# A first x tile loaded entirely by DMA transposes, with W1's row blocks on a second queue

## The chip, the cores and the metric

The kernel runs on one core of one Trainium2 chip. The metric is the device time of one execution in microseconds (us). A core has a matrix engine (TensorE, PE in the profile; its weight loads are the row PEld), a vector engine (VectorE, DVE), an engine for activation functions (ScalarE, ACT), GpSimd (POOL) and SyncE (SP). SyncE, ScalarE and GpSimd each issue DMA transfers from a queue of their own, in program order. An engine runs its own instructions in order too, and waits on semaphores for those of others.

## The reference

The input x has 2048 tokens of 640 features, all in bf16. Three things are computed from it and mixed.

```python
g = _sigmoid((x * gate_w).sum(-1, keepdims=True))
# a: a state space model
dt = jnp.exp(log_dt)
Lam_bar = jnp.exp(dt * Lam)
B_bar = ((Lam_bar - 1.0) / Lam)[:, None] * Bmat
Bu = jnp.einsum("bld,pd->blp", x + 0j, B_bar)
for t in range(L):
    h = Lam_bar[None, :] * h + Bu[:, t, :]
y = 2.0 * jnp.einsum("blp,dp->bld", hseq, Cmat).real + x * Dskip[None, None, :]
# b: a dense layer, GELU, a dense layer
h = _gelu(jnp.einsum("bsd,df->bsf", x, w1) + b1)
b = jnp.einsum("bsf,fd->bsd", h, w2) + b2
return g * a + (1 - g) * b
```

The state has 640 complex values, and w1 is 640 x 1728.

## The kernel before, in words

The tokens are cut into four tiles of 512 (q = 0 to 3). For every tile, x is wanted transposed, with features on the 128 partitions: `xT[q]` holds five slabs (k = 0 to 4) of 128 features x 512 tokens. The other layout, `xn`, has tokens on the partitions, and is used for the gates and for the output.

TensorE does the matrix products: `m1` (x by W1, L670), `bproj` (x by B, L713), `outsT` (the GELU's result by W2, L937, and the state by C, L986), and for the last tile `outs` (L800 and L849). ScalarE applies GELU and moves results out of PSUM, the eight banks that TensorE writes. VectorE builds tables from Lambda and dt, runs the recurrence in blocks of 256 tokens (`ssm`, a scan in L753) and does the final mixing.

The first product, `m1_first` (L648), is special, because nothing is there yet when the kernel starts. It takes the first eight column groups of W1 (jf = 0 to 7, 128 columns each, FW = 1024 columns together), one in each bank, and goes through the features slab by slab: all groups of slab 0, then of slab 1, and so on, 40 products of 128x512, so that it can start with one slab of x and one row block of W1 (`w1load`, 128 x 1024, 256 KB). The product for group 7 of slab 0 stands late in slab 1, because its bank is first used by a small transposition (`cols`, L454). That one turns `rows`, in which the small vectors Lambda, log_dt and b1 lie as rows, into columns; the tables on VectorE and the bias of GELU need it. Its sources are five small loads on ScalarE's queue (`lre`, `lim`, `ldt`, `b1a`, `b1b`).

Ahead of all this, seven products on a constant (`warm`, L415) keep TensorE at work while the first data is on its way.

In the kernel before, slabs 0 and 1 of the first tile come as they lie in memory (`xna`, L369, the first issue of SyncE's queue, 256 KB). TensorE transposes them against an identity matrix (L427, eight instructions of 128x128), VectorE copies the result to `xT[0]` (L433, four copies), and two short products on a constant (`fill`, L440) cover the copies. The first two products are cut in halves of 256 tokens, so that they can start after the first copy. Slabs 2, 3 and 4 are loaded by DMA transposes (`xtrans`, L353), which write `xT[0]` directly. These and all of W1's row blocks stand in SyncE's queue, alternating; the blocks of slabs 1 and 3 are cut in two (WSPLIT). Behind them come the rest of W1 (`w1_r`), B, the other x tiles, W2 and C.

The order of instructions is found by a planner at build time: each operation names its engine, an assumed duration, what it reads and writes, and a priority (lower goes first among what is ready). The planner walks through assumed time and writes one fixed order for each engine. It does not see the chip; a change to one assumed duration or priority can move an instruction in the order.

Of the kernel before, what the change touches and what calls it, by code (L numbers as in the profile page):

```python
# [9 lines left out]
BF16 = mybir.dt.bfloat16  # L10
# [137 lines left out]
class Prog:  # L148
# [8 lines left out]
    def op(self, name, eng, dur, reads, writes, fn, prio=None, lat=0.0, after=()):  # L157
        deps = {}
        for k in reads:
            for w in self.last_w.get(k, ()):  # L160
                deps[w.idx] = w
        for k in writes:
            for w in self.last_w.get(k, ()):
                deps[w.idx] = w
            for r in self.last_r.get(k, ()):
                deps[r.idx] = r
        for a in after:
            deps[a.idx] = a
        deps = list(deps.values())
        E = self.E  # L170

        def run(eg, deps=deps, eng=eng, fn=fn):
            E.wait(eng, *[d.done for d in deps if not (eng == "pe" and d.eng == "pe")])
            return fn()

        it = self.sch.add(name, eng, dur, deps, run, prio=prio, lat=lat)
        for k in writes:
            self.last_w[k] = [it]
            self.last_r[k] = []
        for k in reads:  # L180
            self.last_r.setdefault(k, []).append(it)
        return it


def bass_gated_mix__ssm_conv_s5__dense_activation_gelu__prompt_kernel(
# [18 lines left out]
    _, S, D = A_x.shape  # L204
    P = A_Lambda_re.shape[0]
    F = B_w1.shape[1]
    assert S % 512 == 0 and D % 128 == 0 and P == D
    KD = D // 128
# [6 lines left out]
    FL = F - (NF - 1) * 128  # L215
# [6 lines left out]
    x2 = A_x[0]  # L222
# [3 lines left out]
    with ExitStack() as es:  # L226
# [4 lines left out]
        xT = [SB(f"xT_{i}", [128, KD, 512], BF16) for i in range(NQ)]  # L231
        xn = [SB(f"xn_{i}", [128, 4, D], BF16) for i in range(2)]
        W1sb = SB("W1sb", [128, KD, F], BF16)
# [20 lines left out]
        ident = SB("ident", [128, 128], BF16)  # L254
# [39 lines left out]
        PS = [es.enter_context(nc.psum_tensor(f"ps{i}", [128, 512], FP32)) for i in range(8)]  # L294
# [13 lines left out]
        op = pr.op  # L308

        def inc(eng, ins):  # L310
            return E.inc(eng, ins, eng + "_s")
# [14 lines left out]
        def d_mm(n):  # L326
            return n / 2400.0 + 0.004


        def load(name, eng, sem, dst, src, writes, prio, dur=0.5, lat=2.5, reads=(), after=()):  # L330
            def fn():
                with nc.allow_non_contiguous_dma(reason="columns of small vectors"):
                    return dma_inc(eng, engines[eng].dma_start(dst, src), sem)
            return op(name, eng, dur, reads, writes, fn, prio=prio, lat=lat, after=after)
# [9 lines left out]
        def xnload(q, eng, prio=None):  # L344
            load(f"xn{q}", eng, f"l_xn{q}", xn[q % 2][:, :, :],
                 x2[q * 512:(q + 1) * 512, :].rearrange("(c p) d -> p c d", p=128),
                 [("xn", q % 2, 0), ("xn", q % 2, 1)], prio, dur=1.0, lat=6.0)

        NW = 8
        FW = NW * 128  # L350
        nmain = (NF - 1) * 128

        def xtrans(q, ks, prio, dur):  # L353
            load_T(f"xT{q}_{ks[0]}", f"l_xT{q}_{ks[0]}", [(xT[q][:, ks[0]:ks[-1] + 1, :], x2[q * 512:(q + 1) * 512, ks[0] * 128:(ks[-1] + 1) * 128])],
                   [("xT", q, k) for k in ks], prio, dur)

        WSPLIT = {1: 6, 3: 6}

        def w1load(k, eng, prio):
            edges = [0] + ([WSPLIT[k] * 128] if k in WSPLIT else []) + [FW]  # L360
            for i, (f0, f1) in enumerate(zip(edges, edges[1:])):
                load(f"w1_{k}{i}", eng, f"l_w1{k}{i}", W1sb[:, k, f0:f1], B_w1[k * 128:(k + 1) * 128, f0:f1], [("w1", k, i)], prio=prio + 0.1 * i, lat=2.6)

        def w1tok(k, jf):
            return ("w1", k, int(jf >= WSPLIT.get(k, NW)))

        KN = 2

        load("xna", "sp", "l_xna", xn[0][:, :, 0:KN * 128], x2[0:512, 0:KN * 128].rearrange("(c p) d -> p c d", p=128), ["xna"], 0, dur=0.45, lat=2.0)  # L369
        w1load(0, "sp", 1)  # L370
        w1load(1, "sp", 1.3)
        xtrans(0, range(KN, KN + 1), 1.6, 0.8)
        w1load(2, "sp", 2)
        xtrans(0, range(3, 4), 3, 0.8)
        w1load(3, "sp", 4)
        xtrans(0, range(4, 5), 4.5, 0.8)
        w1load(4, "sp", 5)
        FM = FW + 3 * 128
        for i, (f0, f1) in enumerate(((FW, FM), (FM, F))):
            load(f"w1_r{i}", "sp", f"l_w1r{i}", W1sb[:, :, f0:f1], B_w1[:, f0:f1].rearrange("(k p) f -> p k f", p=128), [("w1", "r", i)], prio=20 + i, lat=5.0)  # L380
# [8 lines left out]
        for i, (nm, (r0, src)) in enumerate(ROWS.items()):  # L389
            src = src.rearrange("(k p) -> k p", p=128)  # L390
            load(nm, "act", "l_" + nm, rows[r0:r0 + src.shape[0], :], src, [nm], prio=-100 + i, dur=0.4)
        load("b1b", "act", "l_b1b", rows[RT:RT + 1, :].rearrange("o (a p) -> o a p", a=2),
             B_b1[nmain:F].rearrange("(o p) -> o p", o=1).unsqueeze(1).broadcast_to([1, 2, FL]), ["b1b"], prio=-101, dur=1.2)

        def f_iota():
            inc("pool", nc.gpsimd.iota(io_i[:, :], pattern=[[1, 128]], base=0, channel_multiplier=-1))
# [14 lines left out]

        def f_warm():
            t = None
            for n in (512,) * 6 + (256,):
                t = nc.tensor.matmul(PS[4][:, 0:n], one.broadcast_to([128, 128]), one.broadcast_to([128, n]), start=True, stop=True)  # L415
            return inc("pe", t)

        op("warm", "pe", 2.7, (), [("bank", 4)], f_warm, prio=-1000)

        for i, (k, c0, c1) in enumerate(((0, 0, 2), (0, 2, 4), (1, 0, 2), (1, 2, 4))):  # L420
            bank = (7, 6, 5, 4)[i]
            pt = PS[bank][:, :].bitcast(BF16)[:, 0:(c1 - c0) * 128]

            def f_xt(k=k, pt=pt, c0=c0, c1=c1):
                t = None
                for c in range(c0, c1):
                    t = nc.tensor.transpose(pt[:, (c - c0) * 128:(c - c0 + 1) * 128], xn[0][:, c, k * 128:(k + 1) * 128], ident[:, :])  # L427
                return inc("pe", t)

            op(f"xt{i}", "pe", 0.11 * (c1 - c0), ["xna", "ident"], [("bank", bank)], f_xt, prio=-990 + i)  # L430

            def f_xc(k=k, pt=pt, c0=c0, c1=c1):
                return inc("dve", nc.vector.tensor_copy(out=xT[0][:, k, c0 * 128:c1 * 128], in_=pt))  # L433

            op(f"xc{i}", "dve", 0.42, [("bank", bank)], [("xT", 0, k, c0)], f_xc, prio=-2000 + i)

        def f_fill():
            t = None
            for _ in range(2):
                t = nc.tensor.matmul(PS[3][:, 0:256], one.broadcast_to([128, 128]), one.broadcast_to([128, 256]), start=True, stop=True)  # L440
            return inc("pe", t)

        op("fill", "pe", 0.22, ["xna", "ident"], [("bank", 3)], f_fill, prio=-900)

        XK0 = [[("xT", 0, k)] for k in range(KD)]
        XK0[0] = [("xT", 0, 0, 0), ("xT", 0, 0, 2)]
        XK0[1] = [("xT", 0, 1, 0), ("xT", 0, 1, 2)]
        XT = {q: [("xT", q, k) for k in range(KD)] for q in range(1, NQ)}
        XT[0] = [t for x in XK0 for t in x]

# [137 lines left out]
        for ci, src in enumerate((A_B_re, A_B_im)):  # L588
            for i, (p0, p1) in enumerate(((0, 512), (512, KP * 128))):
                load_T(f"B{ci}{i}", f"l_B{ci}{i}", [(BT[:, ci, :, p0:p1], src[p0:p1, :])], [("BT", ci, i)], prio=30 + ci + 0.1 * i, dur=0.8 * (p1 - p0) / 128)  # L590
        xtrans(1, range(KD), 32, 3.4)
        load("gwb", "sp", "l_gwb", gwb[:, :], gate_w.partition_broadcast(128), ["gwb"], prio=32.2)
        load("xnb", "sp", "l_xnb", xn[0][:, :, KN * 128:D], x2[0:512, KN * 128:D].rearrange("(c p) d -> p c d", p=128),
             [("xn", 0, 0), ("xn", 0, 1)], 32.4, dur=1.0, lat=6.0, reads=["xna"])
        big = load("w2a", "sp", "l_w2a", W2sb[:, 0:NF - 1, :], B_w2[0:nmain, :].rearrange("(j p) d -> p j d", p=128), ["w2a"], prio=33, lat=8.0)
        load("w2b", "sp", "l_w2b", W2sb[0:FL, NF - 1, :], B_w2[nmain:F, :], ["w2b"], prio=34, lat=4.0)
        load("w2c", "sp", "l_w2c", W2sb[64:64 + FL, NF - 1, :], B_w2[nmain:F, :], ["w2c"], prio=34.2, lat=4.0)
# [12 lines left out]
        def pe_prio():  # L610
            ctr["pe"] += 1
            return ctr["pe"]
# [26 lines left out]
        def m1_first():  # L639
            seq = [(k, jf) for k in range(KD) for jf in range(NW)]  # L640
            seq.remove((0, NW - 1))
            seq.insert(seq.index((1, NW - 1)), (0, NW - 1))
            steps = [(0, 0, 0), (0, 1, 0), (0, 0, 1), (0, 1, 1)] + [(k, jf, None) for k, jf in seq if k or jf > 1]
            for k, jf, h in steps:
                t0, t1 = (0, 512) if h is None else (256 * h, 256 * h + 256)

                def f_mm(jf=jf, k=k, t0=t0, t1=t1):
                    return inc("pe", nc.tensor.matmul(PS[jf][:, t0:t1], W1sb[:, k, jf * 128:(jf + 1) * 128], xT[0][:, k, t0:t1],  # L648
                                                      start=(k == 0 and t0 == 0), stop=(k == KD - 1), skip_group_check=jf < 2))

                op(f"m1_0_{jf}_{k}_{t0}", "pe", d_mm(t1 - t0), (XK0[k] if h is None else XK0[k][h:h + 1]) + [w1tok(k, jf)], [("bank", jf)],
                   f_mm, prio=pe_prio())
            for jf in range(NW):
                ctr["bank"] += 1

                def f_ge(jf=jf):
                    return inc("act", nc.scalar.activation(Gl[0][:, jf, :], PS[jf][:, :], ACT.Gelu_apprx_tanh, bias=b1col[:, jf:jf + 1]))

                op(f"ge_0_{jf}", "act", d_act(512), [("bank", jf), "b1col"], [("gl", 0, jf)], f_ge, prio=10)
# [442 lines left out]
```

## Time and profile before

| | us |
|---|---|
| runs, median of 3 | 213.17 (213.05 to 213.45) |
| profiled execution, first to last instruction (span) | 211.2 |
| TensorE busy | 208.4 (99%) |
| VectorE busy | 190.2 (90%) |
| ScalarE busy | 102.9 (49%) |
| first stage L648, start and end | 4.59 and 13.61 |

The page gives the profiled execution by its span alone; the runs' median is 1.97 us above it. A row of a timeline or of a chain has the start (us from the span's start), the length (us), the engine, and the line of the kernel with what it writes and, after "x", how many instructions are merged. "SPq" and "ACTq" are the queues in which SyncE and ScalarE issue transfers; the length of such a row is the time for issuing, and the time from issue to landing is in a list of its own. In a table by stretches of time, the last three columns are the clock granted to TensorE, the share of time in which DMA packets were under way (it can be over 1), and the GB/s that they moved.

### The profile page before, as it was taken

What the parts mean: (1) busy time and instruction counts of PE and PEld (TensorE: products, weight loads), DVE (VectorE), ACT (ScalarE), POOL (GpSimd) and SP (SyncE); (2) the same over time, 40 slices, a digit from 0 to 9 for tenths busy, and PEclk for the clock granted to TensorE, in tenths of its full rate; (3) what the DMA queues carried; (4) which work ended last, traced back from release to release, by engine and by line L of the source; (5) the groups of instructions that cost most, each with busy time, mean ns of one, the idle gap of its engine ahead of it and who ended that gap; (6) DMA issues with size and microseconds to landing.
All of it is one profiled execution on the core that took longest, in us unless ns stands there. A gap on an engine that the chain in (4) does not pass through costs nothing.

```text
span 211.2 us, 2755 instructions
## 1 busy us (share of the span) xinstructions
PE 208.4 (99%) x1104; PEld 104.3 (49%) x1104; DVE 190.2 (90%) x240; ACT 102.9 (49%) x177; POOL 4.2 (2%) x12
## 2 busy tenths in 40 slices
PE   8999999999999999999999999999999999999996
PEld 3444444444554444444464444444456444567775
DVE  2599999999999999999999999899999999499744
ACT  2588556672990453556680073456660037622330
POOL 1000000030000000000100000000010000000000
PEclk9999999999999999999999999999999999999999
DMA  6899999999930010066074000009542000005251
GB/s 168 203 255 139 193 154 204 310 218 180 218 81 4 0 50 0 0 95 146 10 59 115 3 0 0 0 2 104 114 99 108 0 3 0 0 0 107 69 138 64
DMA packets 48808, 19.08 MB, mean 90 GB/s; under 512 B 41500, under 2 KB 47772, under 8 KB 48796
## 3 DMA queue, kind: packets, MB, share of 16 engines
q1 hardware_dynamic: 47136, 17.59, 41.3%
q0 software_dynamic: 1600, 1.32, 4.5%
q8 instruction: 8, 0.13, 0.3%
q10 hardware_dynamic: 60, 0.01, 0.1%
q14 instruction: 4, 0.03, 0.1%
HBM read 8.41 MB, written 2.63 MB: 52 GB/s over the span
## 4 chain that ended last, share of the span: by engine, by line
PE 99%; DVE 0%; issue 0%
PE ps L670 22%; PE ps L713 20%; PE ps L937 20%; PE ps L986 15%; PE ps L800 7%; PE ps L849 5%; PE ps L648 4%; PE ps L415 1%; PE ps L691 1%; PE ps L948 1%; PE ps L814 0%; PE ps L427 0%; DVE W1sb L883 0%; PE ps L440 0%; PE ps L454 0%
## 5 line engine op out<-in xcount | busy, mean ns | idle before, releaser
L670 PE MATMUL ps<-xT,W1sb 128*128 128x512 bf16 x220 | 48.1, 379 | 0.0
L753 DVE TENSOR_TENSOR_SCAN W<-atab,V 128x1280 bf16<-128x1280 f32 x16 | 44.3, 2812 | 0.3
L713 PE MATMUL ps<-xT,BT 128*128 128x512 bf16 x200 | 43.8, 379 | 0.0
L937 PE MATMUL ps<-Gl,W2sb 128*128 128x512 bf16 (+1 forms) x234 | 42.7, 344 | 0.0
L677 ACT ACTIVATE Gl<-ps,cols 128x512 bf16<-128x512 f32 x44 | 29.9, 694 | 15.5 <-PE ps L670 15.5
L670 PEld LDWEIGHTS ps<-xT,W1sb 128*128 128x128 bf16 x220 | 21.5, 98 | 26.0
L986 PE MATMUL ps<-Hb,CT 128*128 128x512 bf16 x150 | 32.9, 379 | 0.0
L937 PEld LDWEIGHTS ps<-Gl,W2sb 128*128 128x128 bf16 x234 | 22.9, 98 | 19.3
L713 PEld LDWEIGHTS ps<-xT,BT 128*128 128x128 bf16 x200 | 19.5, 98 | 23.8 <-ACT Gt L699 0.4
L722 ACT ACTIVATE U<-ps 128x512 bf16<-128x512 f32 x40 | 23.5, 600 | 14.4 <-PE ps L713 14.3
L955 ACT ACTIVATE E1T<-ps,cols 128x512 bf16<-128x512 f32 (+1 forms) x18 | 9.5, 623 | 33.6 <-PE ps L948 33.6
L986 PEld LDWEIGHTS ps<-Hb,CT 128*128 128x128 bf16 x150 | 14.5, 98 | 17.9 <-DVE V L504 0.6
L994 ACT ACTIVATE E2T<-ps 128x512 bf16<-128x512 f32 x15 | 9.1, 604 | 13.6 <-PE ps L986 13.6
L800 PE MATMUL ps<-W2sb,Gl 128*128 128x320 bf16 x104 | 14.8, 299 | 0.0
L623 DVE SCALAR_TENSOR_TENSOR trf<-xn,gwb 128x640 bf16<-128x640 bf16 x16 | 13.2, 823 | 0.4
L504 DVE TENSOR_TENSOR Hb<-Hb,V 128x1280 bf16<-128x1280 bf16 x16 | 12.5, 822 | 0.3
L504 DVE TENSOR_TENSOR V<-V,W 128x1280 bf16<-128x1280 bf16 x16 | 12.5, 821 | 0.3
L504 DVE TENSOR_TENSOR V<-mr,U 128x2560 bf16<-128x2560 bf16 x8 | 11.9, 1492 | 0.3
L800 PEld LDWEIGHTS ps<-W2sb,Gl 128*128 128x128 bf16 x104 | 10.1, 98 | 4.3 <-issue 0.3
L504 DVE TENSOR_TENSOR Hb<-c,W 128x2560 bf16<-128x2560 bf16 x8 | 11.9, 1490 | 0.2
L974 ACT ACTIVATE xT<-xT,cols 128x512 bf16<-128x512 bf16 x15 | 10.1, 740 | 4.0 <-DMA cols<-in_A_Dskip_dram 4.0
L504 DVE TENSOR_TENSOR W<-mi,U 128x2560 bf16<-128x2560 bf16 x8 | 11.9, 1484 | 0.0
(93 smaller groups left out, 152.0 us busy)
## 6 DMA issues: line engine op xcount, KB each, us to landing
W2sb<-in_B_w_dram SPq DMA_DIRECT2D x1, 2080.0 KB, 9.0
out_dram<-xn SPq DMA_DIRECT2D x3, 640.0 KB, 4.8
xn<-in_A_x_dram POOLq DMA_DIRECT2D x2, 640.0 KB, 7.2
W1sb<-in_B_w_dram SPq DMA_DIRECT2D x3, 256.0 KB, 3.1
trf<-grow SPq DMA_DIRECT2D x3, 256.0 KB, 5.1
xn<-in_A_x_dram SPq DMA_DIRECT2D x1, 640.0 KB, 7.2
W1sb<-in_B_w_dram SPq DMA_DIRECT2D x1, 480.0 KB, 4.0
out_dram<-W1sb SPq DMA_DIRECT2D x3, 160.0 KB, 1.8
```

Of the source, the lines that this page charges most:

```text
L504: return inc("dve", nc.vector.tensor_tensor(out=o, in0=a, in1=b, op=o_))
L623: t = inc("dve", nc.vector.scalar_tensor_tensor(out=scr[:, :], in0=xn[q % 2][:, c, :], scalar=1.0, in1=gwb[:, :], op0=ALU.mult, op1=ALU.mu ...
L670: t = nc.tensor.matmul(PS[bank][:, :], W1sb[:, k, jf * 128:(jf + 1) * 128], xT[q][:, k, :], start=(k == 0), stop=(k == KD - 1))
L677: return inc("act", nc.scalar.activation(Gl[q % 2][:, jf, :], PS[bank][:, :], ACT.Gelu_apprx_tanh, bias=b1col[:, jf:jf + 1]))
L713: t = nc.tensor.matmul(PS[bank][:, :], BT[:, ci, kd, k * 128:(k + 1) * 128], xT[q][:, kd, :], start=(kd == 0), stop=(kd == KD - 1))
L722: return inc("act", nc.scalar.activation(dst, src, ACT.Copy, scale=1.0 if ci == 0 else -1.0))
L753: t = inc("dve", nc.vector.tensor_tensor_scan(out=g[:, ci, :], data0=a, data1=v[:, ci, :], initial=0.0, op0=ALU.mult, op1=ALU.add))
L800: t = nc.tensor.matmul(PS[bank][:, 0:HALF], Gl[q % 2][:, jf, t4 * 128:(t4 + 1) * 128], W2sb[:, jf, cols], start=False, stop=False, skip_gr ...
L849: t = nc.tensor.matmul(PS[bank][:, 0:n], H[b % NHB][:, ci, k, s * 128:(s + 1) * 128], CT[:, ci, k, cols], start=(i == 0), stop=(i == 2 * K ...
L937: t = nc.tensor.matmul(PS[bank][:, 0:t1 - t0], W2sb[:, jf, d * 128:(d + 1) * 128], Gl[q % 2][:, jf, t0:t1], start=(jf == 0), stop=False)
L974: return inc("act", nc.scalar.activation(xT[q][:, d, :], xT[q][:, d, :], ACT.Copy, scale=cols2[:, 1, d:d + 1]))
L986: t = nc.tensor.matmul(PS[bank][:, :].rearrange("p (s t) -> p s t", s=2), CT[:, ci, k, d * 128:(d + 1) * 128], Hb[:, 2 * (q % 2):2 * (q % ...
```

## The change

All five slabs of the first x tile are loaded by DMA transposes from SyncE's queue: three single slabs, then slabs 3 and 4 in one transfer. They are the first four issues of that queue. `xna`, the transposes on TensorE, the copies on VectorE, the filler and the halves are gone; the first stage has 40 whole products. W1's row blocks are whole (no WSPLIT) and go to ScalarE's queue. Its order is now: W1 blocks 0 and 1, `lre`, `lim`, `ldt`, `b1a`, W1 block 2, `b1b`, W1 blocks 3 and 4. The last product of the warm-up has 512 columns where it had 256. The later load of `xn[0]` brings all five slabs (640 KB) where it brought the remaining three (384 KB). The order of TensorE's work is otherwise the same; `cols` stands after 13 instructions of the first stage in both, of which four were halves before.

```diff
-        WSPLIT = {1: 6, 3: 6}
         def w1load(k, eng, prio):
-            edges = [0] + ([WSPLIT[k] * 128] if k in WSPLIT else []) + [FW]
-            for i, (f0, f1) in enumerate(zip(edges, edges[1:])):
-                load(f"w1_{k}{i}", eng, f"l_w1{k}{i}", W1sb[:, k, f0:f1], B_w1[k * 128:(k + 1) * 128, f0:f1], [("w1", k, i)], prio=prio + 0.1 * i, lat=2.6)
+            load(f"w1_{k}", eng, f"l_w1{k}", W1sb[:, k, 0:FW], B_w1[k * 128:(k + 1) * 128, 0:FW], [("w1", k)], prio=prio, lat=2.6)
...
-        load("xna", "sp", "l_xna", xn[0][:, :, 0:KN * 128], x2[0:512, 0:KN * 128].rearrange("(c p) d -> p c d", p=128), ["xna"], 0, dur=0.45, lat=2.0)
-        w1load(0, "sp", 1)
-        w1load(1, "sp", 1.3)
-        xtrans(0, range(KN, KN + 1), 1.6, 0.8)
-        w1load(2, "sp", 2)
-        xtrans(0, range(3, 4), 3, 0.8)
-        w1load(3, "sp", 4)
-        xtrans(0, range(4, 5), 4.5, 0.8)
-        w1load(4, "sp", 5)
+        for ks, prio, dur in (((0,), 0, 1.15), ((1,), 1, 1.15), ((2,), 2, 1.15), ((3, 4), 3, 1.8)):
+            xtrans(0, ks, prio, dur)
+        for k, prio in enumerate((-120, -119, -96, -90, -89)):
+            w1load(k, "act", prio)
...
-             ... ["b1b"], prio=-101, dur=1.2)
+             ... ["b1b"], prio=-95, dur=1.2)
...
-            for n in (512,) * 6 + (256,):
+            for n in (512,) * 7:
...
-            op(f"xt{i}", "pe", 0.11 * (c1 - c0), ["xna", "ident"], [("bank", bank)], f_xt, prio=-990 + i)
...
-            op(f"xc{i}", "dve", 0.42, [("bank", bank)], [("xT", 0, k, c0)], f_xc, prio=-2000 + i)
...
-        op("fill", "pe", 0.22, ["xna", "ident"], [("bank", 3)], f_fill, prio=-900)
...
-        load("xnb", "sp", "l_xnb", xn[0][:, :, KN * 128:D], x2[0:512, KN * 128:D].rearrange("(c p) d -> p c d", p=128),
-             [("xn", 0, 0), ("xn", 0, 1)], 32.4, dur=1.0, lat=6.0, reads=["xna"])
+        xnload(0, "sp", prio=32.4)
...
-            steps = [(0, 0, 0), (0, 1, 0), (0, 0, 1), (0, 1, 1)] + [(k, jf, None) for k, jf in seq if k or jf > 1]
+            for k, jf in seq:
...
+                    return inc("pe", nc.tensor.matmul(PS[jf][:, :], W1sb[:, k, jf * 128:(jf + 1) * 128], xT[0][:, k, :],
+                                                      start=(k == 0), stop=(k == KD - 1)))
```

More of the change, by code (lines that the diff above doesn't have):

```diff
@@ L355, in xtrans @@
                    [("xT", q, k) for k in ks], prio, dur)
-        WSPLIT = {1: 6, 3: 6}
         def w1load(k, eng, prio):
-            edges = [0] + ([WSPLIT[k] * 128] if k in WSPLIT else []) + [FW]
-            for i, (f0, f1) in enumerate(zip(edges, edges[1:])):
-                load(f"w1_{k}{i}", eng, f"l_w1{k}{i}", W1sb[:, k, f0:f1], B_w1[k * 128:(k + 1) * 128, f0:f1], [("w1", k, i)], prio=prio + 0.1 * i, lat=2.6)
+            load(f"w1_{k}", eng, f"l_w1{k}", W1sb[:, k, 0:FW], B_w1[k * 128:(k + 1) * 128, 0:FW], [("w1", k)], prio=prio, lat=2.6)
         def w1tok(k, jf):
-            return ("w1", k, int(jf >= WSPLIT.get(k, NW)))
-        KN = 2
-        load("xna", "sp", "l_xna", xn[0][:, :, 0:KN * 128], x2[0:512, 0:KN * 128].rearrange("(c p) d -> p c d", p=128), ["xna"], 0, dur=0.45, lat=2.0)
-        w1load(0, "sp", 1)
-        w1load(1, "sp", 1.3)
-        xtrans(0, range(KN, KN + 1), 1.6, 0.8)
-        w1load(2, "sp", 2)
-        xtrans(0, range(3, 4), 3, 0.8)
-        w1load(3, "sp", 4)
-        xtrans(0, range(4, 5), 4.5, 0.8)
-        w1load(4, "sp", 5)
+            return ("w1", k)
+        for ks, prio, dur in (((0,), 0, 1.15), ((1,), 1, 1.15), ((2,), 2, 1.15), ((3, 4), 3, 1.8)):
+            xtrans(0, ks, prio, dur)
+        for k, prio in enumerate((-120, -119, -96, -90, -89)):
+            w1load(k, "act", prio)
         FM = FW + 3 * 128
@@ L392, in bass_gated_mix__ssm_conv_s5__dense_activation_gelu__prompt_kernel @@
         load("b1b", "act", "l_b1b", rows[RT:RT + 1, :].rearrange("o (a p) -> o a p", a=2),
-             B_b1[nmain:F].rearrange("(o p) -> o p", o=1).unsqueeze(1).broadcast_to([1, 2, FL]), ["b1b"], prio=-101, dur=1.2)
+             B_b1[nmain:F].rearrange("(o p) -> o p", o=1).unsqueeze(1).broadcast_to([1, 2, FL]), ["b1b"], prio=-95, dur=1.2)
         def f_iota():
@@ L418, in bass_gated_mix__ssm_conv_s5__dense_activation_gelu__prompt_kernel @@
         op("warm", "pe", 2.7, (), [("bank", 4)], f_warm, prio=-1000)
[L420 to L428, printed above, removed]
-            op(f"xt{i}", "pe", 0.11 * (c1 - c0), ["xna", "ident"], [("bank", bank)], f_xt, prio=-990 + i)
-            def f_xc(k=k, pt=pt, c0=c0, c1=c1):
-                return inc("dve", nc.vector.tensor_copy(out=xT[0][:, k, c0 * 128:c1 * 128], in_=pt))
-            op(f"xc{i}", "dve", 0.42, [("bank", bank)], [("xT", 0, k, c0)], f_xc, prio=-2000 + i)
[L437 to L441, printed above, removed]
-        op("fill", "pe", 0.22, ["xna", "ident"], [("bank", 3)], f_fill, prio=-900)
         XK0 = [[("xT", 0, k)] for k in range(KD)]
-        XK0[0] = [("xT", 0, 0, 0), ("xT", 0, 0, 2)]
-        XK0[1] = [("xT", 0, 1, 0), ("xT", 0, 1, 2)]
         XT = {q: [("xT", q, k) for k in range(KD)] for q in range(1, NQ)}
@@ L642, in m1_first, with f_mm @@
             seq.insert(seq.index((1, NW - 1)), (0, NW - 1))
-            steps = [(0, 0, 0), (0, 1, 0), (0, 0, 1), (0, 1, 1)] + [(k, jf, None) for k, jf in seq if k or jf > 1]
[L644 to L652, printed above, removed]
+            for k, jf in seq:
+                def f_mm(jf=jf, k=k):
+                    return inc("pe", nc.tensor.matmul(PS[jf][:, :], W1sb[:, k, jf * 128:(jf + 1) * 128], xT[0][:, k, :],
+                                                      start=(k == 0), stop=(k == KD - 1)))
+                op(f"m1_0_{jf}_{k}", "pe", d_mm(512), XK0[k] + [w1tok(k, jf)], [("bank", jf)], f_mm, prio=pe_prio())
             for jf in range(NW):
```

## The prediction

> **What bounds the kernel now.** First the page's share of busy time and its chain that ended last: TensorE is busy 99% of the 211.2 us, and the chain is TensorE almost alone. So the time is TensorE's work plus whatever it waits at the start; a change at the start counts one for one if nothing later takes it back.
>
> ```profile
> PE 208.4 (99%) x1104; PEld 104.3 (49%) x1104; DVE 190.2 (90%) x240; ACT 102.9 (49%) x177; POOL 4.2 (2%) x12
> PE 99%; DVE 0%; issue 0%
> ```
>
> Then that chain in order of time (start, length, work) shows what the change touches, from the warm-up (L415) to the end of the first stage (L648) at 13.61, where L670 goes on.
>
> ```profile
> 0.78 2.93 PE ps L415 x7
> 3.71 0.04 issue
> 3.75 0.62 PE ps L427 x8
> 4.38 0.22 PE ps L440 x2
> 4.59 2.46 PE ps L648 x13
> 7.05 0.09 PE ps L454
> 7.14 4.53 PE ps L648 x21
> 11.67 0.05 issue
> 11.72 1.89 PE ps L648 x8
> 13.61 5.40 PE ps L670 x25
> ```
>
> The reader is to see that 0.84 us (3.75 to 4.59) go to on-chip transposes and filler, and that the stage then takes 9.02 us. A full-speed 128x512 matmul costs 10.79/50 = 0.2158 us (the L713 run of 50 at 19.00), so 38 of them, four halves and the 0.09 of L454 should take 8.72; about 0.3 us are small waits, the last for W1's fifth block.
>
> Third, the timeline of SyncE's queue: start and length of each issue. One queue issues everything, W1's last block at 8.2.
>
> ```profile
> 0.74 0.46 SPq L333 DMA_DIRECT2D xn<-in_A_x_dram  x1
> 1.26 1.62 SPq L333 DMA_DIRECT2D W1sb<-in_B_w_dram  x3
> 2.92 1.20 SPq L340 DMA_TRANSPOSE xT<-in_A_x_dram  x1
> 4.79 1.13 SPq L340 DMA_TRANSPOSE xT<-in_A_x_dram  x1
> 0.97 1.19 ACTq L333 DMA_DIRECT2D rows<-in_B_b_dram  x1
> ```
>
> The last line is ScalarE's queue: the b1b row is dear to issue; the four other rows take about 0.32 each.
>
> Fourth, time from issue to landing (last number), asked for short windows:
>
> ```profile
> W1sb<-in_B_w_dram SPq DMA_DIRECT2D x1, 256.0 KB, 3.1
> xT<-in_A_x_dram SPq DMA_TRANSPOSE x1, 4.0
> xT<-in_A_x_dram SPq DMA_TRANSPOSE x1, 3.0
> ```
>
> The slab issued at 2.92 took 4.0, behind copies; those at 4.79 and 7.07 took 3.0.
>
> **The change part by part.** The sum is made against the profiled execution: span 211.2; the runs' median of 213.17 is 1.97 more, taken as unchanged around it.
>
> Removed on TensorE: eight transposes and two fillers, 0.84 us on the path. Removed on VectorE: four copies, 0.88 us busy, off the path except for 0.2 us of weight-load wait. Four half matmuls become two whole ones: same columns, nothing.
>
> The warm-up's last matmul grows from 256 to 512 columns. Weight loads of the warm-up are 0.43 us apart, so the seventh starts at 3.34 and leaves at 3.77, before any x can be there: hidden by the wait for x. If x came at 3.74, it would cost 0.03.
>
> Start of real work, t0: the first slab is now the first issue on SyncE, at 0.74 (there is nothing else ahead of it). Landing takes 3.0 (two rows) or 4.0 (one row), so 3.74 to 4.74. I take the middle, 4.24, because W1's first block now moves at the same time, yet no backlog stands ahead as it did in the row of 4.0. W1's first block goes at 0.74 on ScalarE (its first issue no longer waits for the memset of the rows, which held it to 0.97) and lands at 0.74 + 3.1 = 3.84. With the 0.01 from landing to TensorE seen at 3.75, t0 = 4.25; ends 3.85 and 4.75.
>
> The stage: 40 x 0.2158 = 8.63, plus 0.09 for L454, plus 0.05 for joints = 8.77. It ends at 4.25 + 8.77 = 13.02 against 13.61: 0.59 us less. Break-even is t0 = 4.84. The same by parts: 0.84 of transposes and 0.25 of waits go, 0.50 of later start comes (4.25 against 3.75).
>
> Is each operand there? SyncE: 1.15 per slab puts x1's issue at 1.9, x2's at 3.1, the double slab's at 4.3. x1 lands at 4.9 to 5.9, wanted at t0 + 7 x 0.2158 = 5.76: at worst 0.2 lost. x2 lands at 6.1 to 7.1, wanted at 7.8. The double slab: 3.6 by a line from one slab (3.0) to the five-slab load issued at 22.30 (5.3), so 7.9; the upper end is the five-slab load issued at about 32.3 (5.8), so 10.1; wanted at 9.55. I take 7.9, nearest in size; the upper end would lose 0.55. ScalarE: W1 blocks at 0.54 each, rows at 0.34: W1 issues at 0.74, 1.3, 3.2, then b1b at 3.75 to 4.95, then W1 at 4.95 and 5.5. With 3.1 to 3.4 they land at 3.8, 4.4, 6.5, 8.3 and 8.9, wanted at 4.25, 5.8, 7.8, 9.55 and 11.3: hidden by TensorE's own work on the row block before.
>
> A new risk: b1b is now sixth among the small loads and blocks, and L454 (the transpose of the rows) stands in TensorE's order after 13 matmuls, at 4.25 + 2.81 = 7.06. All L648 matmuls behind it would wait. b1b's landing is not shown; by loads (3.0 to 4.0 from issue) it is 6.75 to 7.75, so nothing to 0.7 lost. I take nothing, because it is 0.2 KB. ScalarE's first table load (1.28) moves from 3.58 to about 6.1 and ends at 7.3, while its user waits for L454 until about 7.5: hidden. From VectorE's cast at 7.18 to the end of the GELU table load at 11.36 it is 4.2 us; with the cast at 7.3 the first GELU is out by 12.2, wanted at 13.02.
>
> SyncE's later work (W1's rest, BT, xT1, W2, CT) is issued some 2.7 us earlier, all wanted later than it landed before: nothing. The x load for the gates is 640 KB for 384 KB, at about 23, read at 48.4: hidden by 20 us.
>
> VectorE, 90% busy, is next in line. Its second state block ends at 67.79 and TensorE reads it at 71.71: 3.9 us of room, of which the gain and the later cast take 0.7. At the end, 197.6 against 203.8. So the 0.59 stays: 213.17 - 0.59 = 212.58.
>
> **The rivals.** *Slower: the slabs and W1 share the DMA engines, and the double slab comes late.* All nine loads are now asked for by 6 us, where W1's fifth block alone was issued at 8.2. Before, the first packets moved at about 1.95; W1's 1.31 MB take 3.36 us at the 390 GB/s of the copies at 3.0 to 3.5; five slabs of s each come on top; after the double slab 16 matmuls (3.48 with the joint) remain. The end passes 13.61 when s is over 0.96 us.
>
> ```profile
> 4.75:5.75 1.00, 1.00 (x8) 0.56 (x6) 0.21 (x2) 0.11 (x1) 0.00 (x0) 1.00 1.10 144
> 9.00:10.00 1.00, 1.00 (x6) 0.41 (x5) 0.97 (x3) 0.93 (x3) 0.00 (x0) 1.00 0.70 126
> 32.00:33.50 1.50, 1.50 (x8) 0.69 (x7) 1.47 (x2) 1.11 (x2) 0.00 (x0) 1.00 1.27 290
> ```
>
> Last column GB/s: where a slab of 131 KB passes at the start, 126 to 144 GB/s, s = 0.9 to 1.04; inside a five-slab load 290, s = 0.45. The slow rows are paced by SyncE's 1.13 per issue too, so they bound s from above; but the five-slab load issued at 26.3, mixed with 0.55 MB of copies, landed 8 us after the one before (35.6 and 27.6); less 1.4 for the copies that is 1.3 a slab. At 1.04 the end is 14.0 (+0.4: 213.6); at 1.3 it is 15.3 (+1.7: 214.9).
>
> [...]
>
> *No change: the first slab lands as the one of 4.0 did,* t0 = 4.75: 213.1; or b1b holds L454 by 0.6: 213.2. For it speaks that two queues start together; against it that no backlog is ahead.
>
> *Slower by the clock.* Matmuls run at 0.43 in the warm-up and at 0.2158 later, though the granted clock reads 1.00 throughout. By 3.75 they were fast, with no gap before. Now there is a gap of some 0.5 us before the real work. If it restarted the slow phase for seven matmuls, as many as the warm-up has, that is 7 x 0.21 = 1.48: 214.1. Against it: the warm-up is as long as before. [...]
>
> **How the numbers follow.** Forecast (t0 up to about 4.4, operands in time) 0.45; no change 0.18; shared engines 0.25; clock 0.07; other costs of a queue started with a large block 0.05. A difference under 0.2% (0.43 us) is about what three runs spread over 0.4 us can't tell from none. So faster 0.45, same 0.18, slower 0.37. The likeliest gives 212.6, its own range 212.2 (t0 = 3.85) to 212.8; the range over the cases is 212.1 to 214.3, with the worst of sharing left out.
>
> **What would show it.** Right: no L427, L440 or L433; the chain goes from L415 over a wait for xT of 0.3 to 0.6 us into the first matmuls at 4.1 to 4.4, and L670 begins near 13.0; everything behind moves as a block. Wrong: a wait before the 8th, the 17th or the 25th matmul of the stage (x1, x2, the double slab) that ends with a transpose's landing; a wait at the transpose of the rows; first matmuls 0.43 apart; or a new VectorE wait before L986's counterpart.

## The result, and the profile after

The changed kernel takes 215.76 us (median of 6 runs, 215.53 to 216.86), the kernel before 213.19 in runs alongside it (6 runs, 212.55 to 213.45). The ratio is 1.0124, with a 95% interval of 1.0104 to 1.0145: slower by 1.2%, where 0.3% faster was forecast. The profiled execution of after took 215.65 us, with a span of 214.3.

The page of after, busy shares and the chain's shares by engine:

```profile
PE 208.7 (97%) x1078; PEld 104.1 (49%) x1092; DVE 189.2 (88%) x236; ACT 103.3 (48%) x177; POOL 4.2 (2%) x12
PE 96%; DMA 2%; issue 0%; DVE 0%
```

TensorE has as much work as before and is still the chain; a DMA now holds 2% of it. Where that is, the chain in order of time shows (start, length, work; L607 is the old L648, L416 the old L454, L628 the old L670):

```profile
0.74 5.15 DMA xT<-in_A_x_dram
...
5.94 4.66 PE ps L607 x13
10.60 0.07 PE ps L416
...
10.70 0.20 DVE cols L421
...
10.95 5.79 PE ps L607 x26
16.73 0.22 PE ps L628
```

The second stage begins at 16.73, 3.12 us later than at 13.61 before. Three things differ from the forecast: the first slab is on its way for 5.15 us; the first 13 products take 4.66 us where 13 x 0.2158 is 2.81; and the cast of `cols` on VectorE now stands in the chain. Behind 16.73 everything moves as a block: the last tile's products (L758) begin at 186.58, against 183.46 before, again 3.12 later. By the medians the loss is 2.57 us (215.76 - 213.19); the rest of the 3.12 is the profiled execution of before, which was an early one, as its repeats below show.

The timeline of after (engine and line; in brackets the idle time before, and what ended it):

```profile
0.74 0.87 ACTq L333 DMA_DIRECT2D W1sb<-in_B_w_dram  x2
0.74 5.26 SPq L340 DMA_TRANSPOSE xT<-in_A_x_dram  x4
0.78 3.15 PE L404 MATMUL ps<-const-bfloat16-1.0 128*128 128x512 bf16 x7 [0.78 <-PEq L1045]
5.94 4.66 PE L607 MATMUL ps<-xT,W1sb 128*128 128x512 bf16 x13 [2.02 <-DMA xT<-in_A_x_dram]
8.48 0.15 PEld L607 LDWEIGHTS ps<-xT,W1sb 128*128 128x128 bf16 x1 [0.27 <-issue]
8.90 0.15 PEld L607 LDWEIGHTS ps<-xT,W1sb 128*128 128x128 bf16 x1 [0.28 <-issue]
9.33 0.78 PEld L607 LDWEIGHTS ps<-xT,W1sb 128*128 128x128 bf16 x4 [0.28 <-issue]
10.94 3.14 PEld L607 LDWEIGHTS ps<-xT,W1sb 128*128 128x128 bf16 x16 [0.40 <-DVE cols L421]
```

TensorE idles 2.02 us between the warm-up and the first product, until the slab is there. Then weight loads come 0.43 us apart (8.48, 8.90, 9.33: the pace of the warm-up) until about 9.4, and four in 0.78 us after it. At 10.94 a weight load waits for VectorE's cast.

Landings of the two loads issued at 0.74 (last number: us from issue), then two stretches of the same kernel (last number: GB/s; before it the share of time in which the DMA engines were busy):

```profile
W1sb<-in_B_w_dram ACTq DMA_DIRECT2D x1, 256.0 KB, 2.7
xT<-in_A_x_dram SPq DMA_TRANSPOSE x1, 5.2
```

```profile
1.95:3.75 1.80, 1.80 (x5) 0.45 (x3) 0.00 (x0) 0.00 (x0) 0.00 (x0) 1.00 0.92 282
3.75:5.90 2.15, 0.17 (x1) 0.00 (x0) 0.00 (x0) 0.00 (x0) 0.00 (x0) 1.00 1.01 186
```

The copied block lands first, and the transposed slab that was issued at the same moment lands 2.4 us behind it. In the second stretch the engines are busy for a share of 1.01 on the whole and move only 186 GB/s, where the first had 282 at 0.92; most of its packets are those of slabs (912 of 1070 are of SyncE's queue).

The list of packets by queue adds something. From 1.7 to 2.7 us all 101 packets are those of ScalarE's queue. From 2.7 to 3.6 SyncE's queue moves 512 packets (ScalarE's 82), 0.13 MB, which is one whole slab, and from 3.6 to 4.0 again only ScalarE's queue moves any (79 packets, 0.16 MB). So the slab's packets start about 1 us behind those of W1's first block and are through by 3.6, while its landing comes at 5.89. What holds the landing back for another 2.3 us is not shown.

### The profile page after: what moved, and what is told of

The parts are those of the page before. It is cut to its first block, busy times and chain, and to the rows that moved or that the text cites. A ratio compares the mean times of both kernels' runs of the same rounds, so it can differ in the third digit from the quotient of the medians.

```text
span 214.3 us, 2712 instructions
## 1 busy us (share of the span) xinstructions
PE 208.7 (97%) x1078; PEld 104.1 (49%) x1092; DVE 189.2 (88%) x236; ACT 103.3 (48%) x177; POOL 4.2 (2%) x12
## 4 chain that ended last, share of the span: by engine, by line
PE 96%; DMA 2%; issue 0%; DVE 0%
PE ps L628 22%; PE ps L671 20%; PE ps L895 20%; PE ps L944 15%; PE ps L758 7%; PE ps L807 5%; PE ps L607 5%; DMA xT<-in_A_x_dram 2%; PE ps L649 1%; PE ps L906 1%; PE ps L772 0%; DVE W1sb L841 0%; DVE cols L421 0%; PE ps L416 0%
## 5 line engine op out<-in xcount | busy, mean ns | idle before, releaser
L628 PE MATMUL ps<-xT,W1sb 128*128 128x512 bf16 x214 | 47.5, 379 | 0.3
L671 PE MATMUL ps<-xT,BT 128*128 128x512 bf16 x196 | 43.1, 379 | 0.3 <-issue 0.2
L628 PEld LDWEIGHTS ps<-xT,W1sb 128*128 128x128 bf16 x220 | 21.5, 98 | 26.0
L680 ACT ACTIVATE U<-ps 128x512 bf16<-128x512 f32 x40 | 23.7, 596 | 15.6 <-PE ps L671 15.6
L758 PE MATMUL ps<-W2sb,Gl 128*128 128x320 bf16 x104 | 14.8, 299 | 0.0
L607 PE MATMUL ps<-xT,W1sb 128*128 128x512 bf16 x40 | 10.7, 430 | 2.1 <-DMA xT<-in_A_x_dram 2.0
L466 DVE TENSOR_TENSOR V<-mr,U 128x2560 bf16<-128x2560 bf16 x8 | 11.9, 1492 | 0.3
L758 PEld LDWEIGHTS ps<-W2sb,Gl 128*128 128x128 bf16 x104 | 10.1, 98 | 4.3 <-issue 0.3
L466 DVE TENSOR_TENSOR Hb<-c,W 128x2560 bf16<-128x2560 bf16 x8 | 11.9, 1491 | 0.2
L466 DVE TENSOR_TENSOR W<-mi,U 128x2560 bf16<-128x2560 bf16 x8 | 11.9, 1485 | 0.0
```

Of the source, the lines that this page charges most:

```text
L466: return inc("dve", nc.vector.tensor_tensor(out=o, in0=a, in1=b, op=o_))
L607: return inc("pe", nc.tensor.matmul(PS[jf][:, :], W1sb[:, k, jf * 128:(jf + 1) * 128], xT[0][:, k, :], start=(k == 0), stop=(k == KD - 1)))
L628: t = nc.tensor.matmul(PS[bank][:, :], W1sb[:, k, jf * 128:(jf + 1) * 128], xT[q][:, k, :], start=(k == 0), stop=(k == KD - 1))
L671: t = nc.tensor.matmul(PS[bank][:, :], BT[:, ci, kd, k * 128:(k + 1) * 128], xT[q][:, kd, :], start=(kd == 0), stop=(kd == KD - 1))
L680: return inc("act", nc.scalar.activation(dst, src, ACT.Copy, scale=1.0 if ci == 0 else -1.0))
L758: t = nc.tensor.matmul(PS[bank][:, 0:HALF], Gl[q % 2][:, jf, t4 * 128:(t4 + 1) * 128], W2sb[:, jf, cols], start=False, stop=False, skip_gr ...
```

## The experiments

One relation serves for all of them. In every profiled execution with a time of its own (after, and the eleven below, of both kernels), the time is the start of the second stage (L628 or L670) plus 198.9 to 199.2 us: 215.65 - 16.73 = 198.92 for after. So a variant is read by that start, and nothing behind it matters. By 13.61 + 198.95, the profiled execution of before that the prediction used was one of 212.56, 0.6 us below the median.

**A longer warm-up, nothing else.** Of the kernel after:

```diff
-            for n in (512,) * 7:
+            for n in (512,) * 13:
```

> The changed kernel with a warm-up of 13 instead of 7 products of 128x512, which fills the 2.0 us that TensorE stood idle before the first slab. Theory (the idle time made the real products slow): the first products are 0.2158 us apart at once; the eight that were 0.43 apart give 1.7 us back, of which the late third and fourth row blocks (11.7 to 11.9) keep some 0.4 to 0.6, so the second stage begins at 15.2 to 15.7 instead of 16.73 and the time is about 1.1 to 1.5 us below the changed kernel's, 214.3 to 214.7. Rival (the products become fast at a moment of its own, idle or not, or the first real data makes them slow): still slow products until about 9.4, the second stage at 16.5 or later, 215.5 to 217.

Measured: 215.19 us (214.55 to 215.5), ratio 1.0087 [1.0061, 1.0113]. That is 0.57 us below the changed kernel and lies between the theory's 214.7 and the rival's 215.5. The profiled execution was one of the faster ones, 214.57. Its timeline, and the start of the second stage in its chain:

```profile
0.78 5.00 PE L404 MATMUL ps<-const-bfloat16-1.0 128*128 128x512 bf16 x13 [0.78 <-PEq L1045]
6.35 2.98 PE L607 MATMUL ps<-xT,W1sb 128*128 128x512 bf16 x13 [0.57 <-DMA xT<-in_A_x_dram]
```

```profile
15.66 5.39 PE ps L628 x25
```

The slab landed even later (5.57 us), yet 13 products took 2.98 us in place of 4.66, a rest of 0.17 above 13 x 0.2158: the slow products now lie in the longer warm-up, and none behind it. In this execution the second stage comes 1.07 us earlier. What stays, 2.05 us against 13.61, is the late slab, the wait for the cast and the 0.17 us, a wait for the second slab. By the median only half of the 1.07 us is gained; where the slower executions lose the rest is not shown.

**The same gap in the kernel before.** A warm-up of two products, everything else as before:

```diff
-            for n in (512,) * 6 + (256,):
+            for n in (512,) * 2:
```

> The kernel before with a warm-up of 2 products instead of 7, so that TensorE stands idle from about 1.6 to 3.75, a gap like that of the changed kernel, with everything else as it was. Theory (the gap): products 0.43 apart from 3.75 until some 3 to 3.5 us later, the second stage about 1.2 to 1.7 us later than 13.61, time about 214.4 to 214.9. Rival (fast at a moment of its own near 3.6): no change, 213.2.

Measured: 214.92 us (214.62 to 215.22), ratio 1.0076 [1.0051, 1.0102]. Timeline and chain:

```profile
3.65 1.03 PE L427 MATMUL ps<-ident,xn 128*128 128x128 bf16 x8 [1.86 <-DMA xn<-in_A_x_dram]
```

```profile
5.11 4.64 PE ps L648 x13
...
16.06 5.40 PE ps L670 x25
```

The data is there at 3.65 as ever, but the transposes take 1.03 us where they took 0.62, and the 13 steps that took 2.46 take 4.64; weight loads are 0.43 us apart until about 9.5, which is 5.8 us of slow work and longer than the 3 to 3.5 expected. The time is just above the theory's 214.9 and far from the rival's 213.2. So a short warm-up and a gap of 1.86 us together cost this kernel 1.7 us (214.92 against 213.22 alongside) without any change in its loads; which share each of the two has is not shown.

**What holds the first slab up.** Two variants of the kernel after: in one, every W1 block waits for the first slab; in the other, the later slabs do. (In both, the planner is also told that the first slab lands at once, `lat=0.0`.)

```diff
-    load(f"w1_{k}", ..., prio=prio, lat=2.6)
+    load(f"w1_{k}", ..., prio=prio, lat=2.6, reads=[("xT", 0, 0)])
```

> The changed kernel with W1's five row blocks made to wait for the landing of the first slab, so that only transposes and four rows of a few KB are under way until then. It is a look at the landing, and slower in sum. Theory (W1 on the other queue delays the slab): the first slab lands 3.0 to 3.8 us after its issue instead of 5.2. Rival one (the first transposing load, or several of them one behind the other, are slow by themselves): 4.8 to 5.2 still. Time about 217 to 219.

```diff
-            xtrans(0, ks, prio, dur)
+            xtrans(0, ks, prio, dur, reads=[("xT", 0, 0)] if ks[0] else (), lat=3.0 if ks[0] else 0.0)
```

> The changed kernel with the second to fifth slab made to wait for the landing of the first; W1 goes as in the changed kernel. A look at the landing again. Theory (W1 delays the slab): 4.8 to 5.2 us from issue still. Rival one (the transposes behind it delay it): 3.0 to 4.0. Time 217 to 219, since the later slabs start at 5 to 6.

Measured: 217.7 and 216.54 us, one execution each. Landing of the first slab, first in the kernel whose W1 waits, then in the one whose later slabs wait:

```profile
xT<-in_A_x_dram SPq DMA_TRANSPOSE x1, 2.8
```

```profile
xT<-in_A_x_dram SPq DMA_TRANSPOSE x1, 4.2
```

With W1 out of the way the slab lands in 2.8 us although the other slabs follow it in the queue; with W1 beside it and no slab behind, in 4.2; with both, in 5.2 to 5.6. The 4.2 lies between the theory's 4.8 and the rival's 4.0, so neither is whole: W1 beside it costs 1.4 us, and the later slabs another 1.0 to 1.4, but only where W1 is there too. Both kernels are slower in the end, since what waits comes late. The second showed something else, in its timeline:

```profile
4.98 3.17 PE L607 MATMUL ps<-xT,W1sb 128*128 128x512 bf16 x7 [1.05 <-DMA xT<-in_A_x_dram]
10.02 1.69 PE L607 MATMUL ps<-xT,W1sb 128*128 128x512 bf16 x7 [1.87 <-DMA xT<-in_A_x_dram]
```

Seven slow products (3.17 us), a gap of 1.87 us, then seven fast ones (1.69) at once. So a gap does not by itself bring slow products: here they were slow before it and fast behind it. In the other kernel, whose W1 waits, the products behind a gap of 3.60 us were slow, from 7.53 until about 11.9.

**The kernel before again,** unchanged, twice, to see from when its products are fast.

> The kernel before unchanged, for a second profile of it. The profiled execution that the prediction rests on has a span of 211.2, and other executions of the same kernel 211.3 to 212.3. Theory (the moment from which products are fast differs from run to run, and the forecast rests on an early one, between 3.4 and 3.75): where this profile's span is some tenths longer, its warm-up or first real products are 0.43 apart until a later moment, 4 to 6 us, and the second stage begins as much later than 13.61 as the span is longer than 211.2. Rival (the spread lies elsewhere, in loads or at the end): fast at 3.4 to 3.75 again, the second stage at 13.6, and the difference behind it.

> The kernel before unchanged, a third profile, with the same expectation as for the second: if its span differs from 211.2, the difference stands before the second stage, in products 0.43 apart (theory), or behind it (rival).

Measured: 212.66 and 213.42 us. The two chains:

```profile
3.71 0.89 PE ps L427 x8
...
13.71 5.39 PE ps L670 x25
```

```profile
3.79 1.03 PE ps L427 x8
4.83 0.43 PE ps L440 x2
...
14.22 5.40 PE ps L670 x25
```

The transposes took 0.62 us in the prediction's profile and 0.89 and 1.03 here: the fast pace began near 3.7, 4.3 and 5.5 us in one and the same program, as the theory had it. This moves the second stage by up to 0.6 us, most of the 0.9 us by which these three executions differ (212.56 by the sum above, to 213.42).

**One part of the change at a time.** First all slabs by transposes, but W1's blocks on SyncE's queue between them:

```diff
-        for k, prio in enumerate((-120, -119, -96, -90, -89)):
-            w1load(k, "act", prio)
+        for k, prio in enumerate((0.5, 1.5, 2.5, 3.5, 3.6)):
+            w1load(k, "sp", prio)
```

> One part of the change alone: all five slabs by transposing loads on SyncE's queue, but W1's blocks on the same queue between them (slab, block, slab, block, slab, block, double slab, two blocks). Theory (two queues at once make the first slab late): the first slab lands in 3.0 to 3.6, the first block is issued at 1.9 and sets the start at about 5.0; the slow products are partly hidden by waits for later blocks; the second stage at 14.2 to 15.1, time 213.8 to 215.0, below the changed kernel. Rival (transposing all slabs is the whole cost, whatever the queue): first slab at 5 or more, time 215.5 or more.

Measured: 214.63 us (214.62 to 214.72), ratio 1.0072 [1.0047, 1.0096], a time as the theory had it; the second stage, at 15.69, is later than its 15.1. Landing of the first slab, the timeline of TensorE, and the end of the first stage in the chain:

```profile
xT<-in_A_x_dram SPq DMA_TRANSPOSE x1, 2.7
```

```profile
0.78 2.98 PE L404 MATMUL ps<-const-bfloat16-1.0 128*128 128x512 bf16 x7 [0.78 <-PEq L1045]
5.28 1.67 PE L607 MATMUL ps<-xT,W1sb 128*128 128x512 bf16 x7 [1.52 <-DMA W1sb<-in_B_w_dram]
```

```profile
7.54 4.40 DMA W1sb<-in_B_w_dram
...
12.08 3.61 PE ps L607 x16
15.69 5.40 PE ps L628 x25
```

The slab lands in 2.7 us, the shortest of all (about 0.5 us behind its last packet), but W1's first block now goes out behind it (at 2.03) and sets the start at 5.28; the fourth block is not issued before 7.54, and 16 products wait for it until 12.08. One queue paces these loads too slowly: a slab's issue takes 1.12 to 1.26 us, a block's 0.56 to 0.58. The seven products behind a gap of 1.52 us are fast here (1.67 us). The warm-up's row is 2.98 us for the same seven products that took 3.15 in after, while its weight loads are 0.42 to 0.43 us apart up to the last one listed, at 2.86. By these rows the fast pace seems to have begun in the warm-up's last product; then the gap did not end it. No wait for the cast shows, since the planner put `cols` behind seven products here.

Then the kernel before with W1 on ScalarE's queue, in after's order (and `b1b` moved as there):

```diff
-        w1load(0, "sp", 1)
-        w1load(1, "sp", 1.3)
+        w1load(0, "act", -120)
+        w1load(1, "act", -119)
...
-        w1load(2, "sp", 2)
+        w1load(2, "act", -96)
...
-        w1load(3, "sp", 4)
+        w1load(3, "act", -90)
...
-        w1load(4, "sp", 5)
+        w1load(4, "act", -89)
```

> The other part alone: the kernel before, with W1's blocks (cut as before) on ScalarE's queue in the changed kernel's order; x's first two slabs still as they lie in memory and transposed by TensorE. Theory (sharing): the first load of x, 256 KB beside W1's first blocks, lands in 3.2 to 4.5 instead of 3.0 and the slabs 2 to 4 are asked for earlier and cost W1 and each other time; time 213.2 to 214.5. Rival one (issuing from one queue is what limits the stage): below 212.9. Rival two (W1 on ScalarE's queue is the whole cost): 215 or more.

Measured: 215.12 us (214.03 to 215.71), ratio 1.0082 [1.005, 1.0114]. That is above the theory's 214.5 and inside the second rival's "215 or more". Landing of `xn` (3.0 us before) and the chain:

```profile
xn<-in_A_x_dram SPq DMA_DIRECT2D x1, 256.0 KB, 3.8
```

```profile
4.58 1.04 PE ps L427 x8
...
10.97 0.20 DVE cols L459
...
16.14 5.42 PE ps L670 x25
```

The second queue alone, with no transposed slab at the front, costs two thirds of the whole loss (1.74 of 2.57 us), in the same three ways: a late first load, slow products behind the gap of 0.87 us that this opens (weight loads 0.43 apart until about 8.3), and the wait for the cast. (The planner put `cols` behind 19 instructions here, not 13, so that wait is in part its doing.)

**Fewer blocks beside the slabs.** All slabs by transposes, W1's first block on ScalarE's queue, the others between the slabs; then the third block on ScalarE's queue too:

```diff
-        for k, prio in enumerate((-120, -119, -96, -90, -89)):
-            w1load(k, "act", prio)
+        for k, (eng, prio) in enumerate((("act", -120), ("sp", 0.5), ("sp", 1.5), ("sp", 2.5), ("sp", 3.5))):
+            w1load(k, eng, prio)
```

> A version meant to keep what was good in both: all five slabs by transposing loads, only W1's first block on ScalarE's queue (beside the first slab), the four others on SyncE's queue between the slabs (slab, block 1, slab, block 2, slab, block 3, double slab, block 4). Theory (the more is under way beside the first slab, the later it lands; alone 2.7 to 2.8, with all of W1's issues and the other slabs 5.2): the first slab lands in 3.0 to 3.6, real products start at 3.8 to 4.4 without a gap worth naming, the second stage begins at 13.3 to 14.3, time 212.5 to 213.4, level with the kernel before or a little under it. Rival (one block beside it is enough to delay it by 1.4): first slab at 4.2 or more from issue, start at 4.9 or later, time 214 or more.

> The same with W1's third block on ScalarE's queue too, behind four small rows, so that SyncE's later loads are issued 0.55 us earlier each. Theory: the first slab as in the version with one block; the third block issued at about 3 lands in 3.5 to 4.5 beside two slabs and is not late (wanted near 7.5); second stage at 13.0 to 14.2, time 212.2 to 213.4. Rival (any more on the second queue makes the slabs late): the second or third slab lands 4.5 or more from issue, time 213.5 or more.

Measured: with one block 213.97 us (213.48 to 214.88), ratio 1.0035 [1.0019, 1.0051]; with two 214.65 (214.19 to 215.61), 1.0083 [1.006, 1.0107]. The intervals don't overlap, so moving one more block beside the slabs, with SyncE's later loads issued earlier by it, costs about half a per cent. In the profiles the first slab lands in 3.8 and 3.6 us; with two blocks the second slab takes 5.0. With one block the measured values lie between theory and rival, in landing (3.6 and 4.2) and in time (213.4 and 214); with two, it is the rival that came true. The timeline with one block:

```profile
0.78 3.15 PE L404 MATMUL ps<-const-bfloat16-1.0 128*128 128x512 bf16 x7 [0.78 <-PEq L1045]
4.63 5.17 PE L607 MATMUL ps<-xT,W1sb 128*128 128x512 bf16 x13 [0.70 <-DMA xT<-in_A_x_dram]
```

A gap of only 0.70 us, and 13 products take 5.17 us. This was the slowest execution of that kernel (214.88).

**The gap filled and the cast covered.** The kernel with one block beside, with nine warm-up products and `cols` planned two products earlier:

```diff
-            for n in (512,) * 7:
+            for n in (512,) * 9:
...
-        op("cols", "pe", 0.3, list(ROWS) + ["b1b", "ident"], [("bank", 7)], f_cols, prio=13.5)
+        op("cols", "pe", 0.3, list(ROWS) + ["b1b", "ident"], [("bank", 7)], f_cols, prio=11.5)
```

> Edit: all five slabs by transposes, W1's block 0 alone on ScalarE's queue, the other blocks on SyncE's between the slabs, as in the version with one block beside; new: nine warm-up products in place of seven, and the transposition of the rows planned two products earlier. Theory (the three costs of the change are the late first slab, the slow products after the unfilled wait, and the wait for the cast at bank 7): the first slab still lands 3.7 to 4.0 us from issue, the warm-up now ends near 4.6 and leaves no gap, the products are 0.22 us apart from 5.5 at the latest, the wait for the cast is under 0.1 us, the second stage begins at 13.4 to 14.5 (15.9 with the gap), and the median is 212.6 to 213.6, level with the kernel before. Rival (the gap has no part in it, and the slow phase lasts to about 9 us whenever the slabs come as transposes): weight loads 0.43 us apart until about 9 us, second stage from 15.5 on, median 213.9 or more.

Measured: 213.77 us (213.1 to 214.5), ratio 1.0041 [1.002, 1.0061], 0.17 us above the end of what the theory gave; the rival's 213.9 lies close, but not its slow products. Timeline, then the end of the stage in the chain:

```profile
4.59 2.57 PE L607 MATMUL ps<-xT,W1sb 128*128 128x512 bf16 x11 [0.33 <-DMA xT<-in_A_x_dram]
7.05 2.97 PE L607 MATMUL ps<-xT,W1sb 128*128 128x512 bf16 x13
```

```profile
6.47 4.09 DMA xT<-in_A_x_dram
...
10.61 3.70 PE ps L607 x16
14.31 5.42 PE ps L628 x25
```

In this profile no product behind the warm-up is slow, none waits for the cast, and the first slab lands in 3.8 us. What is left is the loads: the stage waits at each new slab, and at last for the double slab, which lands at 10.56; 16 products remain behind it, and the second stage begins at 14.31. But the profile (213.26) is at the lower end of this kernel's runs, as that of the kernel with one block was at the upper end, and by the medians the two don't differ: the intervals overlap. Its fast pace also began near 3.6, inside the first seven products, so this execution had little need of the two that were added. What the gap costs there is shown in single executions and not in the median. No version tried here beats the kernel before.

## Why the prediction was wrong

**What failed.** The sum was 13.02 for the start of the second stage; it was 16.73. Three steps make up the difference.

- *"t0 = 4.25"* The first product began at 5.94: +1.69. The step took the middle of 3.0 and 4.0 us for the landing "because W1's first block now moves at the same time, yet no backlog stands ahead". The backlog was beside it, not ahead: the slab takes 2.7 to 2.8 us with no block of W1 beside it, 3.6 to 3.8 with one or two on the other queue, 4.2 with W1 as in after and no later slab, 5.2 to 5.6 with the later slabs too. The bounds came from rows in which one queue issued everything, and such rows can't contain this. The rival of shared engines had loads of the two queues delay each other, but looked for it at the double slab and not at the first one.
- *"The stage: 40 x 0.2158 = 8.63, plus 0.09 for L454, plus 0.05 for joints = 8.77."* It took 10.79. Eight of the first products were 0.43 us apart and not 0.2158: about +1.7. The rival of the clock had this with seven (1.48 us) and got a chance of 0.07. The reason given against it, that the warm-up is as long as before, failed: in before, work follows the warm-up with a gap under 0.1 us, and in its three profiles the fast pace sets in only at the warm-up's end (3.71) or behind it, near 3.7, 4.3 and 5.5 us, under the transposes and first products. In after, work stops at 3.93 with the pace still slow, and 2.02 us without work follow.
- *No wait at `cols`.* This was missed. The step looked at what L454 waits for (`b1b`), not at who waits for it. The product for group 7 of slab 0 needs bank 7 back, so it waits for VectorE's cast of the transposed rows. In before, 13 instructions ahead of `cols` are 11 products, and three more stand between it and that product; in after they are 13, and only one stands between. It starts at 10.50 and the one that waits at 10.95, 0.23 us more than the usual 0.2158.

13.02 + 1.69 + 1.7 + 0.23 = 16.64, against 16.73; the remaining 0.09 is not assigned. The 1.7 is that of the profiled execution: by the median the longer warm-up gave back 0.57 us of it.

**The double slab** was taken to land at 7.9. It was issued at 4.68 and landed at 12.1 (the expectation for the longer warm-up had 11.7), and W1's last block landed at 12.6 in place of 8.9. Neither shows as a wait in after, because the products were late by then; nor is there one in the profile of the longer warm-up, whose first slab was later still. But 16 products behind 12.1 end at 15.6 at the earliest. By 15.6 + 198.95 the kernel could not have been below 214.5 with these loads, near that rival's upper price of 214.9. The sum's third assumption, operands in time, failed as well, then, without being what set the time. What the rival said of the loads agrees with the first slab's landings (2.7 us with W1 behind it in its own queue, 5.2 beside the other queue's) and with the packets of after: from 2.7 to 3.6 us those of SyncE's queue took 63.5% of the 16 engines' time and those of ScalarE's 42.3%.

**"1.97 more, taken as unchanged around it."** 1.3 us lies around the span (215.65 against 214.3). The other 0.6 was a profiled execution with an early fast pace. It did not move the difference that was forecast, but it hid that the pace of the first products varies.

**What held.** The transposes, fillers and copies are gone. `b1b`'s landing, the table load and SyncE's later work cost nothing. VectorE's room of 3.9 us was never used up; the loss passes one for one to the end.

**What stays open.** Why the fast pace sets in when it does. Runs of unbroken work became fast 2.8 to 4.7 us after their start at 0.78 (the filled version and the second repeat of the kernel before; the ends are read from where the pace of the rows changes). Work behind a gap in a slow warm-up took 2.2 us (two blocks beside) to 5.8 us (the warm-up of two products). The moment varies, then (near 3.7, 4.3 and 5.5 us in one program). A gap of 2.02 us behind a slow warm-up had eight slow products behind it; gaps of 0.33 and 0.57 us behind warm-ups that had turned fast (nine and thirteen products) had none; and in one kernel the pace turned within a gap of 1.87 us. What sets the moment is not shown by any run. Also open is why the first slab's landing comes 2.3 us behind its last packet when copies and more slabs are under way.

## What to carry to other kernels

A warm-up whose fast pace has not yet begun can be lost to a gap behind it: cut to two products, with a gap of 1.86 us, it cost the kernel before 1.7 us. Judge its length by the time at which data comes in the new schedule, with some to spare, since the moment of the fast pace moved by almost 2 us between three executions of one program (near 3.7, 4.3 and 5.5 us); and judge what it brings by medians, since single profiles showed more than the medians did (1.07 against 0.57 us for the longer warm-up). Moving W1 to a second queue made its issue earlier but not its landing: the fifth block was issued at 5.4 and landed at 12.6, where before it was issued at 8.2 and landed 3.4 us later. What lands first was then no longer chosen by the order of one queue (W1's first block in 2.7 us, the slab issued with it in 5.2), so keep the load that starts the chain ahead of the others in one queue, or without others beside it (2.7 and 2.8 us here), and count what their later issue costs. The landing times of the schedule with one queue, 3.0 to 4.0 us, were no bound for the one with two, 5.2.

## What the runs showed of the hardware

- In after, a transposing load of 128 KB and a copy of 256 KB, issued at the same moment on two queues with more of each behind them, landed in 5.2 and 2.7 us; the same transposing load landed in 2.7 when the copies stood behind it in its own queue. In the first case its 512 packets are through 2.3 us before it counts as landed, in the second about 0.5 us.
- In after, from 3.75 to 5.90 us, while slabs were transposed beside copies, the DMA engines show a busy share of 1.01 at 186 GB/s; in the stretch just before (1.95 to 3.75) they moved 282 at 0.92.
- Products turned fast during a gap in one kernel (3.17 us for seven ahead of 1.87 us of idle time, 1.69 behind it); in another, seven took 1.67 us behind a gap of 1.52. The granted clock reads 1.00 in after up to 13 us and in the first of these kernels from 7 to 11 us, over slow and fast products alike, so the slow pace is seen only in the distances between instructions and in their lengths (634 ns against 379 for a product of after).
- Two executions of one program (212.66 and 213.42 us) differ by when TensorE turned fast, and with it the second stage's start, 13.71 and 14.22.
